# A new global order and new buffer slots for the tasks of an attention and feed-forward kernel

## The chip, the cores and the metric

One core of a Trainium2 chip. The time of a run is the device time of one execution in microseconds. In the profile PE is TensorE (PEld its weight loads), DVE is VectorE, ACT is ScalarE, POOL is GpSimd and SP is SyncE, which here does nothing but start transfers.

## The reference

Attention over 4 batches, 8 heads, 768 positions and 64 dimensions per head, and on its result x (3072 tokens of 512 features) a gated feed-forward layer of width 1536:

```
mask   = causal                         for heads 0, 2, 6
       = causal and (in the last 64 or among the first 4)   for the others
a      = softmax(mask(q k^T / 8));   x = a v, heads side by side
g      = x @ w_gate;   gelu = 0.5 g (1 + erf(g / sqrt(2)))
ffn    = (gelu * (x @ w_val)) @ w_out
out    = x + sigmoid(x @ w_res) * ffn
```

## The kernel before

The 3072 tokens are worked in six chunks of 512 (CHUNKS, called chunk 0 to 5; a chunk may join the end of one batch and the start of the next). For a chunk, q, k and v are loaded by POOL's queue with a cast to 16 bits (`ld`, line 539). Features of q and k are brought onto the partitions by TensorE transposes and a copy for the first chunks (`qkT` line 682, `qkE` line 693), by DMA transposes on SP's queue for the later ones (`dT`, line 726); some of the results are copied once more by SP (`q6`, line 737), and parts of v too (`vs`, lines 617 and 633). Then come the scores (line 850), exp on ACT (line 866), masks on DVE (line 902), the products with v (lines 477, 478, 974) and the division by the row sum (`rcp` line 1028, `norm` and `norm16` lines 1039 to 1048), which gives x twice, in 32 and in 16 bits. x is turned to features by TensorE (`xT`, line 1063, and a copy `xE`, line 1071) and, in one block of chunks 3 to 5, by a DMA transpose on SP's queue (`xD`, line 1054). Gate and value products (`g`, `v`) follow, erf-gelu and product (lines 1098 to 1228), and the products with w_out (`fw`; for part of the gate, value and w_out products sums of blocks are formed first, so that seven products do the work of eight; lines 1151 to 1331), the residual gate (`res`, `tanh` line 1299), `gated` (line 1355), `add` (line 1365) and the output. In chunks 1 to 4, x itself is stored first (`xst`, line 1281, SP) and the rest is added to it in memory by an accumulating transfer of POOL (`out`, line 1359); a buffer of x is written again only after its store.

Matmul helper lines: 477 uses the whole array; 478 works in two halves of 64 columns, two instructions for one of line 477. Which form is used follows from the mode of the array where a task stands.

All of this is a graph of 1861 numbered tasks. `schedule()` does not search: it goes through the list PLAN, one global order in which each number is a task, and appends the task to the list of its engine. A letter behind a number picks the engine where a task may run on several (a ACT, d DVE, g POOL, s SP). `wN` stands for N fillers: matmuls of 128x256 on a zero tile whose result nobody reads (line 1414). PLACES says for each buffer, in the order of the tasks, which slot of its pool it takes; a task that takes a slot waits for the users of the buffer that had it. `assign_waits()` derives the semaphore waits, and each engine then runs its list strictly in order:

```
for x in "".join(PLAN).split():
    if x[0] == "w":
        for _ in range(int(x[1:])):
            t = next(fillers)
            t.bufs[0].fixed = t.bufs[0].pool.quiet("warm")
            if t.bufs[0].fixed is not None:
                place(t, "pe")
    else:
        t = self.tasks[int(x.rstrip("padgs"))]
        place(t, {"p": "pe", "a": "act", ...}[x[-1]] if x[-1] in "padgs" else t.eng)
```

Some numbers used below: 0 to 17 constants and masks; 199 to 204 the thirds of w_gate and w_val, 205 w_res, 206 to 209 w_out; 210 to 215 q and k of chunk 0, 216 to 219 its v; 244, 245, 254, 255 q and k of chunk 1; 302 a `dT` and 334, 335 `q6` copies of chunk 3; 522 and 538 gate matmuls of chunk 0; 973 `xst` of chunk 2; 1175, 1181, 1199 `norm` and `norm16` tasks of chunk 3, 1201 and 1203 its `xT`, 1183 its `xD`; 1819, 1851 and 1852 final `add` tasks.

Of the kernel before, what the change touches and what calls it, by code (L numbers as in the profile page):

```python
# [51 lines left out]
    "1 0 14 214 16 210 211 212 215 2 5 w39 240 213 241d w2 228 216 229a w4 230 236 231d 217 237d w6 411 3 6 232 412 4 233d "  # L52
    "200 w4 408 242 409 7 w1 234 243d 238 8 235a 9 239d 10 219 w5 414 410 w1 476 415 11 222 425 416 223 419 224d 426 221 "
    "420 417 422 218 418 225d 427 428 478 421 459 423 477 220 429 424 199 430 w3 442 460 443 413 471 444 431 245 445 432 "
    "472 w1 449 446 447 433 450 255 451 464 462 448 465 434 452 201 453 463 w4 467 461 202 13 435 468 w4 455 436 479 480 "
    "481 466 203 457 456a 437 w1 438 440 458a 482 439d 204 441d w1 473 226d w1 523 474 483 454 205 539 484 538 475 254 227d "
    "522 485 244 503 470 524 505 469 504 540 252 525 207 506 486 541 496 253a 497 488 507 498 206 499 487 514 500 489 501 "
    "266 516 490 17 530 491 267a 256 494 511 531 495d 246 532 492 515 493d 208 502 509 546 508 510a 552 512d 247 533 534 "
    "517 554 209 536 527 556 257 542 558 268 547 548 280 553 550 281 549 526 551 269 555 528 570 529 535 543 537 572 15 576 "
    "594 574 578 544 588 580 545 577 598 559 557 571 590 582 573 584 575 579 586 561 560 564 562 610 592 563 566 581 264 "  # L60
    "568 250 611 265d 296 518 290 589 520 251d 565 287 567 519 289 569 262 198 690 521 295 687 691 12 679 248 591 599 259a "
    "277 680 583 593 585 276 602 688 621 597 293 587 612 622 332 689 670 261a 676 671 674 326 600 249 613 605 623 283 675 "
    "260d 606 624 603 677 625 272 682 595 626 271 681 685 667 601 686 683 284 668 607 672 678 263 614 292 615 684 669 627 "
    "274 632 628 673 616 275 609 617 629 322 692 696 618 697 636 286 633 638 637 634 693 640 639 604 694 641 635 695 698 "
    "714 715 699 642 608 643 258d 700 644d 713 645a 703 701 704 705 649 706 702a 646 707 647 716 718 596 650 648a 709 708 "
    "717 711 710a 652 719 651 722 720 723 653 712d 724 721a 655 725 656 654 740 726 741 727 730 658 731d 728 659 657 729a "
    "747 619 746 660 620 735 770 734 630 742 736 664 631 771 737 273 738 772 752 661 744 754 739 743 662 748 732 745 774 "
    "750 278 663 749 756 775d 785 270 773 776a 777 751 786a 753 787a 755 778 282 796 779 797a 788 781 758 789 799 297 798a "
    "760 800 790 782 792 780 294 757 801 784 793 791 803 783 802 795 285 804 759 794 806 807 762 761 291 808d 805 818 763 "
    "809a 810 829 819d 288 764 811 830a 820d 821 398 831a 812 822 832 813 814 279 328 823 833 824 299 825 306 834 815 298 "  # L70
    "836 835 329 816 826 837 827 848 817 300 828 838 766 320 849 839 765 768 307 767 665 931 397 769 850 343 840 932 852 "
    "844 853 304 851 841 922 856a 924 308 906 845 925 858 847 859 309 843 854 860a 855 842 301 923 864 857d 865 316 846 910 "
    "907 866 926 861 870 911 871 862 914 927 863 928 875 867 929 874 868 909 876 881 310d 908 915 917 912 869 317 882 877 "
    "913 916 342 918 872 934 935 303 936 937 920 878 919 331 942 933 921 938 879 873 939 940 885a 943 323 944 318 880 887 "
    "945 888 946 941a 325 956 952 883 889a 930 957 958 319 884 947 948 953 333 959 949a 954 955 950 960 963 951a 961 965 "
    "315 964 893 886a 966 962a 894 967 330 890 312a 891 313d 895 971 892 969 972a 899 968 666 896 970a 314 897 900 305 976 "
    "1011 981 898 975 327 977 978 979 982 302 980 984 988 311d 1013 983 1012 1015 324 1014 985 987 986 989 990 345 1016d "
    "991 1026 973 992 1018 1027a 993 1017a 995 334 1019 1029 321 904 997 1037 1020 1038a 1021 1022 1028a 994 1030 1039a "
    "1023 903 1040 1024 1031 905 1041 996 1025 1032 998 1042 1048 1033 1000 1044 335 1049a 1034 1045 1035 1043 999 1036 "
    "1046 1051 1001 1047 1050d 1059 1052 1003 1070 1060d 1002 901 1061a 1062 1071a 1054 902 1063 1072a 1005 1004 1064 360 "  # L80
    "1073 1066 1053 1065 1074 336 1007 1055 1075 337 1056 1077 1067 1076 1058 1068 371 1078 1089 1069 1079 347 1009 1057 "
    "1006 1090 358 1008 1080 733 1091 369 1010 384 1166 1081 1093 1167 383 1085 1094 1082 1092 1153 400 1151 1097d 1154 "
    "1159 1095 1086 357 1099 1084 1152 1100 1083 361 1096 1101a 1156 1088 1098a 1163 394 1157 1087 1105 1106 404 1102 1164 "
    "1107 1103 1158 1111 1112 1160 1104 1147 1116 1161 1115 1108 1148 1109 1155 1117 1118 1110 1162 1149 340 1188 1150 1177 "
    "1119 1168 1113 349 1178 1122 1165 1173 1169 1170 1171 350 1179 1172 1189 1184 1185 1120 1174 1180 368 1175 1123 1181 "
    "372 1121 1186 1190 1195 1126d 401 1191 365d 1187 1176d 1124 1125 1192 1114 1183 1182 1197 1128 1127a 1129 1193 1196 "
    "1131 1130a 1198 1132 1194a 370 1199 1134 1135 1133 1203 1136 1201 338 1137 1204d 1202a 1138 1140 1139 1141 1200 1219 "
    "373 1214 1142 1208 1243 1143 1213 359 1145 1220 1245 339 1244 1215 1216 1217 346 1207 1218 1221 354 1222 1246 1223 "
    "1209 355 1210 1224 1211 385 1231 1212 1258 395 1269 1259a 1247 348 1270a 1225 1260a 1248d 1271a 1227 1249d 1250 344 "
    "1272 1251 1261 1233 1273 367 1252 1262 1235 1253 1254 351 1263 1144 1264 1265 1255 1274 1257 1226 366 1276 1266 1206 "  # L90
    "1256 1275 399 1268 1229 1228 1267 1280 1277 341 1281d 1237 1279 1230 1239 974 1282a 1291 1278 352 1283 1238 1292a 1284 "
    "356 1302 1293d 1294 1303a 1285 1295 1240 1241 1205 1287 1305 1304a 1296 1242 1286 353 1306 1288 380 1297 1298 1308 "
    "1289 376 1307 1299 1309 1321 1146 1301 1290 1300 1310 379 1232 1322 1312 1234 388 1311 1402 1323 392 1236 1403 1317 "
    "403 1325 1313 1324 1326 377 363d 1387 1314 1329a 1385 1399 1386 1327 1318 1388 1331 364d 1316 1332 1328 1320 1400 "
    "1333d 1379 1383 1315 1337 1330a 374 1380 1338 1319 1334 381 1401 1335 1384 1339 1393 1390 1381 1343 1336 396 1391 1344 "
    "1382 1404 1340 1348 1405 362a 1389 1406 1394 378 1407 1408 1409 1341 1410 1354 1411 1355 1413 1342 405 1412a 1397 "
    "1358d 1395 1392 1415 1396 1414 1356 1416 1360 1417 1361 1398 1357 1347 1419 1420 1424 1362d 1359a 1349 1425 1418 1421 "
    "1422 1423 1426 1427 1366 1428 1363 1429 375 1367 1364 1430a 1368 1431 1365 1432 1433 1372 1434 1369 1435 1370 1373 "
    "1371 1437 1439 1438a 1350 1440d 1436 1444 1351 1481 1450 1345 1452 1374 1455 1346 1443 1479 513 1445 391 1446 1447 382 "
    "1449 1448 1461 1375 1451 1480 1457 1453 389 1483 1454 1463 1484a 1456 1459 1485d 1486 1465 1458 1487 1679 1494 1442 "  # L100
    "1460 1462 1495a 1482 1488 1464 1490 1489 1496d 1491 1466 1497 1493 1505 390 1498 1467 1492 1499 1506a 1469 1501 386 "
    "1508 1507d 1471 1500 1509 1441 1502 1516 1503 402 1510 1517a 1511 1504 1518a 1468 1512 1519 393 1527 1520 1470 1528a "
    "1513 1529a 1472 1521 1530 387 1515 1522 1523 1514 1473 1531 1524 1538 1525 1533 1539a 1526 1475 406 1532 1540d 1477 "
    "1541 1474 1534 407 1542 1476 1535 1543 1536 1352 1545 1537 1478 1544 1353 1549 1640 1546 1377 1557 1376 1548 1378 1641 "
    "1559 1547 1558 1550 1633 1560 1621 1631 1553 1634 1561 1552 1562 1563 1554 1565a 1564 1556 1632 1567 1551 1568 1566d "
# [1405 lines left out]
```

## Time and profile before

| | |
|---|---|
| median of 3 runs | 266.2 us (265.41 to 267.15) |
| profiled execution | 264.3 us, span from its first to its last instruction |
| granted TensorE clock, mean | 0.997 |
| PE busy | 254.5 us (96%), 3421 matmuls |
| DVE busy | 210.8 us (80%), 473 instructions |
| ACT busy | 155.3 us (59%), 274 instructions |
| POOL busy | 106.8 us (40%), 145 instructions |

The profiled execution has its span as its only time. Busy time counts an engine's computation; issuing a DMA counts on POOL and not on SP. Times are microseconds from the span's start; a matmul of a row x8 is one of eight that overlap, so the step from one to the next is shorter than its duration.

### The profile page before, as it was taken

How to read it: one execution, taken by the hardware profiler on the slowest of the kernel's cores; microseconds unless marked ns; L12 is line 12 of the kernel's file. 1: busy time of each engine (PE TensorE's matmuls, PEld its weight loads, DVE VectorE, ACT ScalarE, POOL GpSimd, SP SyncE). 2: the span in 40 equal slices, each digit the busy share in tenths (PEclk: the TensorE clock that was granted, in tenths of full speed). 3: DMA queues.
4: the chain of work that ended last, by engine and by line, in shares of the span. 5: the costliest groups of instructions: out<-in, count | busy, mean ns of one | idle time of the engine just before them, and what ended most of it. 6: DMA issues, size and time to landing. Idle time of an engine off the chain costs nothing.

```text
span 264.3 us, 8077 instructions
## 1 busy us (share of the span) xinstructions
PE 254.5 (96%) x3421; PEld 180.7 (68%) x3421; DVE 210.8 (80%) x473; ACT 155.3 (59%) x274; POOL 106.8 (40%) x145
## 2 busy tenths in 40 slices
PE   8999999999999999999998899999999998999993
PEld 5657655558567578667677477579588677778891
DVE  1499555999988978678999677999687976877985
ACT  1277534964554998564883356884655995445511
POOL 8996741990000998013976620711500111110021
PEclk9999999999999999999999999999999999999998
DMA  7999999999297999968999994899589509050004
GB/s 69 166 139 178 207 196 191 188 158 115 82 271 99 141 123 135 182 154 182 136 97 124 152 138 93 200 123 104 69 92 237 101 2 122 7 77 2 2 2 159
DMA packets 102067, 33.17 MB, mean 125 GB/s; under 512 B 88720, under 2 KB 97168, under 8 KB 102032
## 3 DMA queue, kind: packets, MB, share of 16 engines
q0 software_dynamic: 74704, 18.88, 77.3%
q1 hardware_dynamic: 26896, 13.26, 25.0%
q8 instruction: 27, 0.44, 0.7%
q10 hardware_dynamic: 432, 0.52, 0.5%
q14 instruction: 8, 0.07, 0.1%
HBM read 29.36 MB, written 10.49 MB: 151 GB/s over the span
## 4 chain that ended last, share of the span: by engine, by line
PE 87%; DVE 8%; DMA 3%; issue 1%; ACT 0%; DVEq 0%
PE ps L477 45%; PE ps L478 30%; PE ps L850 4%; PE ps L1414 4%; DMA xT<-x 3%; PE ps L682 2%; PE ps L974 2%; PE ps L1063 1%; DVE xtok L1041 1%; DVE x L1039 1%; DVE vk L598 1%; PE ps L941 1%; DVE hS L1251 0%; DVE hT L1228 0%; DVE vs L617 0%
## 5 line engine op out<-in xcount | busy, mean ns | idle before, releaser
L539 POOL DMA_DIRECT2D qks<-in_q_dram x37 | 33.2, 983 | 48.3 <-DMA qT<-qks 26.1
L1359 POOL DMA_DIRECT2D out_dram<-otile x16 | 15.6, 975 | 76.8 <-DVE otile L1355 66.2
L477 PE MATMUL ps<-xT,wg 128*128 128x512 f16 (+1 forms) x172 | 38.7, 337 | 1.4 <-DMA xT<-x 1.0
L477 PE MATMUL ps<-xT,wv 128*128 128x512 f16 (+1 forms) x172 | 38.5, 337 | 0.0
L1129 ACT ACTIVATE gact<-ps 128x512 f16<-128x512 f32 x38 | 22.1, 596 | 27.0 <-PE ps L477 18.0
L1131 DVE SCALAR_TENSOR_TENSOR hT<-gact,ps 128x512 f16<-128x512 f16 x38 | 25.8, 683 | 13.7 <-ACT gact L1129 5.8
L539 POOL DMA_DIRECT2D qks<-in_k_dram x37 | 34.8, 977 | 1.4 <-POOLq L1493 0.8
L1203 DVE TENSOR_TENSOR ps<-ps,otile 128x256 f32<-128x256 f32 x60 | 24.0, 428 | 7.7 <-PE ps L477 3.7
L1221 ACT ACTIVATE gact<-ps 128x512 f16<-128x512 f32 x30 | 16.6, 596 | 15.7 <-PE ps L477 10.8
L539 POOL DMA_DIRECT2D va<-in_v_dram x24 | 23.7, 1017 | 3.8 <-DVE va L534 3.8
L477 PEld LDWEIGHTS ps<-xT,wg 128*128 128x128 f16 x172 | 16.2, 98 | 13.1 <-DMA xT<-x 1.5
L477 PEld LDWEIGHTS ps<-xT,wv 128*128 128x128 f16 x172 | 16.6, 98 | 11.4 <-issue 0.2
L866 ACT ACTIVATE ea<-ps 128x1024 f16<-128x1024 f32 (+2 forms) x24 | 22.0, 925 | 1.4 <-PE ps L850 1.3
L1228 DVE SCALAR_TENSOR_TENSOR hT<-gact,ps 128x512 f16<-128x512 f16 x30 | 19.3, 682 | 2.6 <-PE ps L478 1.2
L1299 ACT ACTIVATE srs<-ps 128x512 f32<-128x512 f32 x22 | 13.1, 599 | 12.2 <-PE ps L478 7.8
L477 PE MATMUL ps<-wo,hT 128*128 128x256 f16 (+1 forms) x114 | 18.3, 296 | 0.0
L478 PE MATMUL ps<-xT,wg 128*64 128x512 f16 (+1 forms) x144 | 17.6, 344 | 0.0
L478 PE MATMUL ps<-xT,wv 128*64 128x512 f16 (+1 forms) x144 | 17.6, 344 | 0.0
L1041 DVE TENSOR_TENSOR xtok<-ps,rcp 128x512 f32<-128x512 f32 (+1 forms) x28 | 16.8, 608 | 0.6
L1331 DVE TENSOR_TENSOR otile<-otile,ps 128x256 f32<-128x256 f32 x33 | 13.1, 412 | 3.7 <-PE ps L477 2.4
L850 PE MATMUL ps<-qT,kT 64*128 64x64 f16 (+4 forms) x391 | 15.9, 213 | 0.1
L478 PE MATMUL ps<-wo,hT 128*64 128x256 f16 x216 | 15.6, 273 | 0.4 <-DVE otile L1325 0.4
(175 smaller groups left out, 590.4 us busy)
## 6 DMA issues: line engine op xcount, KB each, us to landing
out_dram<-xtok SPq DMA_DIRECT2D x4, 1024.0 KB, 4.8
out_dram<-otile POOLq DMA_DIRECT2D x16, 256.0 KB, 4.5
va<-in_v_dram POOLq DMA_DIRECT2D x24, 128.0 KB, 5.6
qks<-in_k_dram POOLq DMA_DIRECT2D x32, 64.0 KB, 4.9
qks<-in_q_dram POOLq DMA_DIRECT2D x32, 64.0 KB, 5.0
wv<-in_moe_w_val_dram POOLq DMA_DIRECT2D x3, 512.0 KB, 13.2
wg<-in_moe_w_gate_dram POOLq DMA_DIRECT2D x3, 512.0 KB, 11.4
wo<-in_moe_w_out_dram POOLq DMA_DIRECT2D x4, 384.0 KB, 20.9
```

The lines of the kernel that those rows point to most:

```text
L477: return e.matmul(o, lhsT=lhsT, rhs=rhs, **k)
L478: return [e.matmul(o[h:h + 64], lhsT=lhsT[:, h:h + 64], rhs=rhs, **k) for h in (0, 64)][-1]
L539: return G.add(eng, issue, lambda e: e.dma_start(out_ap(), in_ap), deps, prio, bufs=bufs, dma=cost, name=name, grp=grp)
L850: return [e.matmul(at(scr)[:, oo:oo + w], lhsT=side(BB, qb, low, 1)[half, k0:k0 + 128], rhs=side(BB, qb, low, 0)[half, qq:qq + w], start=T ...
L866: return e.activation(out=o, in_=i_, func=AF.Exp, scale=SM_SCALE)
L1041: t2 = G.add("dve", c_dve(2 * n * 64), lambda e: e.tensor_tensor(out=xview(), in0=avv(0, DHEAD), in1=scale(), op=ALU.mult), [t1] + xdeps, ...
L1129: ta = G.add("act", c_act(512), (lambda gb=gb, ga=ga, gw=gw: lambda e: e.activation(out=at(ga)[:, :], in_=at(gb)[:, gw], func=AF.Gelu))(), ...
L1131: th = G.add("dve", c_dve(512), (lambda vb=vb, ga=ga, f=f, vw=vw: lambda e: e.scalar_tensor_tensor(out=hv(f), in0=at(ga)[:, :], scalar=0.5 ...
L1203: return G.add("dve", c_dve(256), lambda e: e.tensor_tensor(out=at(ps)[:, o], in0=at(ps)[:, BL], in1=at(es)[:, 0:256], op=ALU.add), deps, ...
L1221: ta = G.add("act", c_act(512), (lambda x=x, ga=ga, both=both: lambda e: e.activation(out=two(at(ga)[:, :]), in_=both(x), func=AF.Gelu))() ...
L1228: th = G.add("dve", c_dve(512), (lambda x=x, f=f, ga=ga, both=both: lambda e: e.scalar_tensor_tensor(out=two(hv(f)), in0=two(at(ga)[:, :]) ...
L1359: t = G.add("pool", 1.0, (lambda ot=ot, r0=r0: lambda e: e.dma_start(out[r0:r0 + 128, :], at(ot)[:, :], accum_op=ALU.add))(), ends + [stor ...
```

## The change

PLAN and PLACES are replaced; nothing else in the program differs. Both orders contain the same numbered tasks except for fillers. In words of the order: 48 fillers in place of 77, the first group 25 in place of 39. The list of loads on POOL has another order: the loads of q and k of chunk 1 (244, 245, 254, 255) all stand ahead of the weights 201 to 205. Of SP's transfers, `xst` of chunk 2 (973) and the `dT` and `q6` of chunk 3 (302, 334, 335) come later in the order, and of the two DVE tasks that feed `xD` (1183) the last is now 1181 (`norm16`) and was 1176 (`x16`, a cast). Of the final additions two (1819, 1851) run on DVE in place of POOL. DVE has ten instructions fewer, ACT 13 more, POOL two fewer, SP one fewer. 28 more value matmuls and 16 more residual-gate matmuls are in the two-halves form (14 and 8 fewer in the full form).

```diff
--- before.py
+++ after.py
@@ -49,85 +49,84 @@
...
 PLAN = (
-    "1 0 14 214 16 210 211 212 215 2 5 w39 240 213 241d w2 228 216 229a w4 230 236 231d 217 237d w6 411 3 6 232 412 4 233d "
-    "200 w4 408 242 409 7 w1 234 243d 238 8 235a 9 239d 10 219 w5 414 410 w1 476 415 11 222 425 416 223 419 224d 426 221 "
-    "420 417 422 218 418 225d 427 428 478 421 459 423 477 220 429 424 199 430 w3 442 460 443 413 471 444 431 245 445 432 "
-    "472 w1 449 446 447 433 450 255 451 464 462 448 465 434 452 201 453 463 w4 467 461 202 13 435 468 w4 455 436 479 480 "
-    "481 466 203 457 456a 437 w1 438 440 458a 482 439d 204 441d w1 473 226d w1 523 474 483 454 205 539 484 538 475 254 227d "
-    "522 485 244 503 470 524 505 469 504 540 252 525 207 506 486 541 496 253a 497 488 507 498 206 499 487 514 500 489 501 "
-    "266 516 490 17 530 491 267a 256 494 511 531 495d 246 532 492 515 493d 208 502 509 546 508 510a 552 512d 247 533 534 "
...
-    "1011 981 898 975 327 977 978 979 982 302 980 984 988 311d 1013 983 1012 1015 324 1014 985 987 986 989 990 345 1016d "
-    "991 1026 973 992 1018 1027a 993 1017a 995 334 1019 1029 321 904 997 1037 1020 1038a 1021 1022 1028a 994 1030 1039a "
...
-    "1119 1168 1113 349 1178 1122 1165 1173 1169 1170 1171 350 1179 1172 1189 1184 1185 1120 1174 1180 368 1175 1123 1181 "
-    "372 1121 1186 1190 1195 1126d 401 1191 365d 1187 1176d 1124 1125 1192 1114 1183 1182 1197 1128 1127a 1129 1193 1196 "
-    "1131 1130a 1198 1132 1194a 370 1199 1134 1135 1133 1203 1136 1201 338 1137 1204d 1202a 1138 1140 1139 1141 1200 1219 "
...
-    "1801 1835 1803a 1834d 1804 1789 1836 1805 1837a 1838 1806d 1839 1793 1807 1840 1841 1842 1849 1844 1851g 1843 1808 "
...
-    "1818 1812 1819g 1797 1816 1859a 1817 1821 1822 1820s 1823d 1824a "
+    "0 212 198 213 1 14 16 17 215 2 w25 234 232 233 235a w5 414 419 416 5 210 420 415 211 w5 228 229a w3 230 238 242 243a "
+    "214 6 217 231 15 216 408 239 409 245 236 237a 240 241 3 411 412 422 423 459 7 460 218 8 4 225 9 410 244 10 467 11 224 "
+    "425 426 418 427 219 428 429 417 430 w5 476 220 468 w2 471 199 478 421 477 424 413 431 472 221 464 449 461 223 442 432 "
+    "226 465 222 443 450 451 444 445 200 473 433 469 474 434 462 446 452 447 435 255 463 w3 252 453 436 448 254 227a 438 "
+    "466 439 470 250 440 454 496 441 475 251a 437 457 458a 479 201 203 455 480 497 498 253a 456 499 481 500 482 503 504 501 "
+    "483 522 502 484 530 505 506 204 485 202 524 538 532 486 507 487 488 489 514 511 490 531 516 205 257 540 512 509 510 "
+    "492 493 539 494 533 246 247 523 525 495a 266 508 518 520 541 491 515 517 256 534 543 542 526 264 536 265 544 528 267a "
+    "207 519 535 521 558 537 560 562 527 679 206 680 13 545 12 208 209 546 564 570 588 572 576 574 552 577 579 566 578 580 "
+    "290 554 590 559 561 529 581 563 594 589 591 571 592 556 598 573 575 593 289 346 286 582 548 259 584 568 674 667 296 "
+    "550 636 583 565 586 567 569 585 587 668 675 553 676 677 339 295 269 337 261 262 248 690 691 271 555 557 547 549 669 "
...
+    "1067 305 318 382 1073 1072 352 994 996 1068 1069 302 1147 1074 1148 1075 998 1076 397 335 1089 1090 1077 1078 1091 "
+    "1092 1081 1082 1079 1080 1156 1157 1161 1085 376 1093 1094 905 342 379 377 902 1162 334 1084 1083 1095 1096 1163 1166 "
...
+    "1110 1113 1190 513 1116 973 1173 400 1197 1185 1174 1155 1186 1187 1191 1118 1119 358 1120 380 1198 388 1121 1175 1122 "
+    "366 1176 1177 1192 1179 1123 1178 1193 1199 1180 1181 1124 1125 1126a 1127 1128 1129 1194a 1203 1117 367 1183 1200 "
...
+    "1845 1846 1805 1847 1806a 1848 1810 1809 1850 1811 1813 1794 1795 1852g 1856 1851 1858 1860 1814 1796 1797 1854a 1812 "
+    "1816 1817 1815 1818 1819 1853a 1822 1821 1820a 1823 1824a "
 )
 PLACES = (
...
 )
...
```

## Rows read from the trace of the kernel before

**Rows 1.** the page: busy time of the engines; the chain that ended last
```profile
PE 254.5 (96%) x3421; PEld 180.7 (68%) x3421; DVE 210.8 (80%) x473; ACT 155.3 (59%) x274; POOL 106.8 (40%) x145
...
PE 87%; DVE 8%; DMA 3%; issue 1%; ACT 0%; DVEq 0%
```

**Rows 2.** five stretches: busy us of each engine (instructions), PEclk, DMA share, GB/s
```profile
13.70:23.70 10.00, 9.30 (x152) 5.96 (x151) 9.56 (x29) 7.84 (x17) 9.96 (x14) 1.00 1.43 145
23.70:124.00 100.30, 100.30 (x1054) 65.88 (x1055) 81.31 (x184) 63.57 (x111) 43.29 (x56) 1.00 1.35 165
124.00:150.00 26.00, 24.23 (x305) 17.07 (x303) 22.02 (x49) 15.88 (x25) 19.59 (x26) 1.00 1.46 115
150.00:262.00 112.00, 108.16 (x1781) 82.91 (x1779) 93.65 (x205) 64.51 (x118) 21.82 (x27) 1.00 0.61 92
220.00:227.00 7.00, 5.94 (x200) 5.76 (x196) 4.90 (x12) 2.86 (x6) 0.00 (x0) 1.00 0.65 88
```

**Rows 3.** PE's timeline of the start: start us, us, work, [idle before <- releaser]
```profile
1.21 7.03 PE L1414 MATMUL ps<-blank 128*128 128x256 f16 x39 [1.21 <-DVE blank L511]
...
23.67 0.71 PE L477 MATMUL ps<-xT,wg 128*128 128x256 f16 x5 [0.38 <-DVE xtok L1041]
```

**Rows 4.** line 1414 up to 8.2 us: ns min/median/max of one
```profile
L1414 PE MATMUL ps<-blank x39: 272/421/421, 1.2 to 8.0; 128*128 128x256 f16 x39
```

**Rows 5.** DVE's timeline of the start, columns as in rows 3
```profile
14.61 0.52 DVE L508 COPY m_win<-m_win 128x256 f16<-128x256 f16 x1
...
23.10 0.42 DVE L1041 TENSOR_TENSOR xtok<-ps,rcp 128x256 f32<-128x256 f32 x1
```

**Rows 6.** POOL's timeline of the start
```profile
11.36 0.24 POOL L497 TENSOR_SCALAR_AFFINE_SELECT m_win<-m_win 128x64 f16<-128x64 f16 x1
11.55 0.91 POOL L539 DMA_DIRECT2D va<-in_v_dram  x1
...
14.79 0.75 POOL L539 DMA_DIRECT2D wg<-in_moe_w_gate_dram  x1
```

**Rows 7.** tile wg: us from issue to landing of its loads
```profile
DMA to landing us min/median/max: 7.5/11.4/15.0
```

**Rows 8.** the chain that ended last, in order of time, before chunk 3
```profile
141.80 0.64 DVE x L1048
142.46 7.36 DMA xT<-x
```

**Rows 9.** PE's timeline of the hand-over to chunk 3
```profile
143.20 0.82 PE L477 MATMUL ps<-wo,hT 128*128 128x256 f16 x6
144.74 0.61 PE L1063 MATMUL ps<-ident,x 128*128 128x128 f16 x8 [0.72 <-DVE x L1039]
...
149.86 0.61 PE L477 MATMUL ps<-xT,wg 128*128 128x512 f16 x2 [1.05 <-DMA xT<-x]
```

**Rows 10.** line 1054, the DMA transposes of x: us from issue to landing
```profile
DMA to landing us min/median/max: 3.7/4.9/7.4
```

**Rows 11.** SP's queue from 112 to 125 us
```profile
113.50 2.58 SPq L726 DMA_TRANSPOSE kT<-qks  x2
...
116.82 0.59 SPq L1281 DMA_DIRECT2D out_dram<-xtok  x1
```

**Rows 12.** PE's timeline around 223 us
```profile
223.98 0.44 PE L478 MATMUL ps<-vk,ek 128*64 128x65 f16 x16 [1.06 <-issue]
```

**Rows 13.** all engines' timeline of the tail
```profile
258.99 1.27 POOL L1365 TENSOR_TENSOR otile<-otile,xtok 128x512 f32<-128x512 f32 x1 [1.96 <-DVE otile L1355]
...
260.91 0.69 DVE L1365 TENSOR_TENSOR otile<-otile,xtok 128x512 f32<-128x512 f32 x1
```

**Rows 14.** the longest waits: engine, line <- releaser: us in total, times, longest
```profile
POOL out_dram L1359 <- DVE otile L1355: 66.2, 8, 15.9
```

**Rows 15.** PE's timeline of chunk 3's first scores
```profile
130.67 0.27 PE L850 MATMUL ps<-q 64*128 64x256 f16 x1
```

123 rows, old and new, of tables (PLACES, PLAN) are left out of this document.

## The prediction

> **What bounds the kernel now.** I read four views. First the busy totals and the chain that ended last [rows 1]: PE is busy 254.5 of 264.3 us, and 87% of the chain is PE. Both orders hold the same real tasks, so most of the time can't move. Second the stretches [rows 2]: PE is full from 23.7 to 124 us, loses 0.7 us between 13.7 and 23.7, 1.8 us around the change from chunk 2 to chunk 3 (124 to 150), and 3.8 us in all of 150 to 262. Third the timelines of what loses, by the idle time in brackets before PE's groups: 1.21 us at the start and 0.38 before the first gate matmul [rows 3], 0.72 and 1.05 at the hand-over to chunk 3 [rows 9], 1.06 at 223.98 [rows 12]; and in the tail 2.7 us of a last DMA after DVE's last addition, 260.91 + 0.69 = 261.60 [rows 13]. Fourth the fillers (line 1414), 77 of them, which keep PE at work where it would wait [rows 3, 4]; the new order has 48. A filler that covers a wait costs nothing by itself, but what shortens the wait lets it be dropped. So what an order can win is some of the 8 us of fillers at the start and 4 to 5 us of gaps; and any new wait between 23.7 and 124 us is paid whole.
>
> The sum is made against the profiled execution, 264.3 us, and 1.9 us are added for the median (266.2).
>
> **The start.** The first gate matmul of chunk 0 stands at 23.67 us, behind a DVE normalisation that began at 23.10 and ended at 23.52 [rows 3, 5]. DVE is busy 9.56 of the 10 us before [rows 2]; its chain from the mask copy of line 508 (14.61) to that norm is 23.52 - 14.61 = 8.9 us [rows 5]. The new order cuts the first fillers from 39 to 25. The 39 take 7.03 us [rows 3]: 25 slow ones (421 ns long [rows 4], a step of 0.21) and 14 fast ones (272 ns, a step of 0.11), so 25 end at about 6.5 us instead of 8.2. But DVE's chain is fed by the mask constants from POOL, of which the last ended at 11.36 + 0.24 = 11.60 [rows 6]. In the new order 11 loads are issued ahead of it instead of 9, at 0.75 to 0.91 us each [rows 6]: 11.60 + 2 x 0.85 = 13.3 us. From there the DVE tasks in front of the first gate matmul (now task 522) add up to 9.4 us by the durations that the same tasks had, so it comes at some 22.8 us, 0.8 us earlier. Ahead of it PE has done 0.7 us more real work than before (transposes and scores of chunk 1), which is saved later. Together **-1.5 us**. Bounds: -2.5, if DVE's chain isn't held by the constants; +0.5, if the landing of the first gate weights decides: their load was issued at 14.79 [rows 6] and the quickest of the three took 7.5 us [rows 7], so 22.3, only 1.4 us ahead of its use.
>
> **The weights behind it.** Two more loads of q and k of chunk 1 (254 and 244, 256 KB each) now stand ahead of the weights 201 to 205: 0.5 MB at 165 GB/s [rows 2] is 3.1 us of stream. Against it, the PE work ahead of each weight's first use grows by about as much, since PE does chunk 1's transposes earlier. Counted by bytes ahead and work ahead, each weight lands 1.3 to 3 us before its use; I put it at **0**, bounds 0 to +3, since PE has nothing else in line to hide a late weight behind.
>
> **The hand-over to chunk 3.** Before, PE stood 0.72 us for x of line 1039 and 1.05 us for the DMA transpose of x (line 1054) [rows 9], which was issued at 142.46 after a cast on DVE and took 7.36 us in the chain [rows 8]. The three of this kind took 3.7, 4.9 and 7.4 us [rows 10]. In the new order the feeder on DVE (1199) of the TensorE transposes (1203, 1201) is ahead of the other norm, and four final matmul groups lie in front of them: I let the 0.72 go whole. The DMA transpose (1183) now follows norm16 1181, DVE's sixth task after the norm 1175: 0.64 for the cast [rows 8], about 0.65 for each of three norms and 0.15 for each of two reciprocals, 2.9 us. PE reaches the last task that feeds 1181 about 1.05 us after 1175, so 1181 ends 1.85 us after that task. From there PE has 12 final groups of three matmuls (a step of 0.11 each, 0.33 a group [rows 9]), two transposes (0.22 each) and six gate and value groups (0.43 each) before it needs the result: 7.0 us. Less DVE's 1.85 that is 5.2 us. With a transfer of 4.9 us nothing waits; with 7.4 it is 2.2 us. I take 0.7, as many of POOL's loads have left that stretch: 1.77 becomes 0.7, **-1.1**, bounds -1.8 and +0.4.
>
> The shortest of the three transposes, 3.7 us, lies in a stretch in which POOL is busy 0.00 us; around the longest POOL is busy 19.59 of 26 us [rows 2, 10]. A rule of the Trainium skill ("DMA: Bandwidth & Descriptors", Issuing engines are not separate DMA queues) says that transfers run on the same 16 engines and interleave, whichever engine issued them; with that the trace agrees, and by the rule alone the emptier stretch would win the whole 1.77.
>
> **Later gaps.** The 1.06 us at 223.98 waited for nothing that the profile shows ("issue") [rows 12]; I take it as an even chance that it comes back somewhere. The 0.7 us of other small gaps behind DVE should be less, as DVE loses ten tasks and ACT gets 13. **-0.6**, bounds -1.5 and +0.3. The DMA transposes of chunks 4 and 5 have 7.2 and 7.5 us of PE work after their feeders, before 7.4 and 7.9: no wait at 3.7 to 4.9 us and 1 to 1.5 us of DVE.
>
> **The tail.** Two of the final additions move from POOL (1.27 us for 512 columns) to DVE, where one takes 0.69 [rows 13]. After PE's last matmul DVE has one addition more: **+0.3**, bounds 0 and +0.7.
>
> **Forms.** 28 more value matmuls and 16 more of the residual gate run on halves of the array, two for one, in place of 14 and 8 on the whole. Laid end to end by the steps that the tasks had, the real PE work is 241.9 us against 241.3: **+0.6**, bounds 0 and +1.
>
> **New waits.** 1861 tasks have new places, and the old order shows that several gaps of 0.2 to 1 us stay in one that looks smooth. **+0.6**, bounds 0 and +2 (one more hand-over like the old one).
>
> Sum: -1.5 + 0 - 1.1 - 0.6 + 0.3 + 0.6 + 0.6 = -1.7 us: span 262.6, median **264.5 us**. The terms' ends don't all meet; this case has 262.8 to 266.2 as its own range.
>
> **Rivals.** (1) *All gaps close*: start -2.5, hand-over -1.8, later gaps -1.2, no new wait: -2.5 - 1.8 - 1.2 + 0.3 + 0.6 = -4.6, **261.6 us**. Against it is DVE's chain at the start, which stays.
>
> (2) *It does not do what it says*: the transpose at the hand-over takes 7.4 us whatever lies beside it, so 2.2 us of wait (+0.4), and the start gains only the 0.7 us of work moved forward, no gap closes: +0.4 - 0.7 + 0.3 + 0.6 + 0.6 = +1.2, **267.4 us**; with new waits at 0, 266.8.
>
> (3) *Slower, by SP's queue before chunk 3.* Transfers of SP start in line. A copy of q (334) waits for a transpose (302) that was issued in the pair at 113.50 [rows 11]; the first scores of chunk 3 that read such a copy ran at 130.67, 14 us later [rows 15]. In the new order 302 waits for a load that stands on POOL behind two output transfers, and those wait for DVE (8 such waits, the longest 15.9 us [rows 14]). By the tasks ahead I place its landing at 120 to 122 us and the first scores of chunk 3 at 125 to 126: 3 to 6 us of room. The store of chunk 2's x (973), for which a norm of chunk 3 waits, is behind it. From a delay of 4.5 us on, each further us stands on PE. A POOL wait longer by half of that longest one, 8 us, gives 3.5 us: 266.2 + 3.5 less the 0.3 or so that the rest then still gains, **269.4 us**.
>
> (4) *Slower, by the clock.* The granted clock is 1.00 from 13.7 to 262 us, the 2.4 GHz level [rows 2]; but the first fillers ran 421 ns and the later ones 272 [rows 4], so PE began at 1.2 GHz and rose while 39 fillers stood back to back. Now 25 stand there, as many as were slow, and behind them come transposes and gaps. If the clock rises only with the dense matmuls, the 8 to 9 us of real work in the start take twice as long; some 5 us of fillers and waits take up the rest: +4 us on the forecast, **268.5 us**.
>
> On this the Trainium skill ("TensorE: Matmul & The Clock Gate", Part 4: PE-mode transpose) speaks against the change: a transpose on TensorE does not count as busy in the same way, so it does not raise the clock. In the trace of before the clock had risen ahead of the first transpose; no row here shows either.
>
> **Chances.** Forecast 0.48, rival 1 0.13, rival 2 0.20, rival 3 0.12, rival 4 0.07. A measurement of this kernel tells some 1% (2.66 us) from no change: faster is below 263.5, slower above 268.9. Faster: 0.13 and half of the forecast's case, 0.24: 0.37. Slower: rivals 3 and 4, less a little: 0.18. Within 1%: 0.45. The range goes from rival 1's middle (261.5) to short of rival 3's (269.0).
>
> **What would show it.** The first gate matmul at 22.5 to 23 us behind DVE; fillers of 272 ns before 9 us; PE full from there to 120 us; under 1 us idle at the hand-over and the transpose of x under 6 us; DVE's last addition 1.6 to 1.9 us after PE's end. The prediction is wrong if PE waits for a weight between 30 and 55 us, for a copied q or a norm at 120 to 140 us, or if the clock stays low.

## The result and the profile after

The changed kernel is slower: 269.86 us median of 16 runs against 265.54 for the kernel before, 1.0163 times as long by these medians, 1.0118 (interval 1.0089 to 1.0147) by the ratio without outliers; in a second series of runs 1.0207 (1.0155 to 1.0259). Every ratio with an interval leaves out the runs that lie over 1.5% above the fastest of the same kernel as disturbed, and since this kernel spreads from 266.6 to 273.6 us (and once 510), such a ratio is more a lower bound here, and the ratio of the medians of all runs stands beside it where the argument hangs on it. The profiled execution is one of the quick ones: 267.34 us, span 265.6, against a median of 266.2 and a span of 264.3 for the kernel before.

The page of the changed kernel, the lines that answer to [rows 1] (its line numbers are one lower):

```profile
PE 253.5 (95%) x3414; PEld 176.5 (66%) x3414; DVE 204.8 (77%) x463; ACT 163.0 (61%) x288; POOL 104.6 (39%) x143
...
PE 76%; DMA 11%; DVE 6%; SPq 3%; POOL 1%; issue 1%; ACT 0%; POOLq 0%; DVEq 0%
```

PE is busy 1.0 us less, and yet the kernel is slower. The chain names the new part: DMA has 11% of it in place of 3%, SP's queue 3% in place of nothing. The stretches, the same ones as in [rows 2], and one of 3.3 us behind the hand-over:

```profile
13.70:23.70 10.00, 8.64 (x172) 6.08 (x173) 9.88 (x34) 8.40 (x15) 9.87 (x16) 1.00 1.61 187
23.70:124.00 100.30, 99.33 (x1006) 63.89 (x1004) 77.31 (x172) 66.23 (x117) 51.70 (x67) 1.00 1.57 169
124.00:150.00 26.00, 24.02 (x318) 16.95 (x315) 20.39 (x46) 16.31 (x27) 17.91 (x22) 1.00 1.44 138
150.00:262.00 112.00, 110.24 (x1785) 81.97 (x1785) 92.21 (x202) 65.72 (x119) 12.65 (x15) 0.98 0.45 77
150.50:153.80 3.30, 3.30 (x10) 1.20 (x8) 1.71 (x5) 1.19 (x2) 0.65 (x2) 0.50 1.04 178
```

PE is no longer full between 23.7 and 124 us, where POOL and the DMA engines are busier (DMA share 1.57 against 1.35), and behind the hand-over the granted clock is 0.50, 1.2 GHz, for a while. Such a stretch can't be seen in busy time, where PE looks full: 10 matmuls ran in it. PE's timeline at three places, the start, a new wait and the hand-over:

```profile
1.13 5.52 PE L1413 MATMUL ps<-blank 128*128 128x256 f16 x25 [1.13 <-DVE blank L510]
...
22.92 1.04 PE L476 MATMUL ps<-xT,wg 128*128 128x256 f16 x8
```

```profile
97.26 1.89 PE L476 MATMUL ps<-wr,xT 128*128 128x512 f16 x8
100.09 0.22 PE L973 MATMUL ps<-vs,es 128*64 128x65 f16 x1 [0.94 <-DMA vs<-va]
```

```profile
150.11 0.76 PE L476 MATMUL ps<-xT,wg 128*128 128x512 f16 x2 [2.09 <-DMA xT<-x]
150.67 1.06 PE L476 MATMUL ps<-xT,wv 128*128 128x512 f16 x2
151.52 1.91 PE L476 MATMUL ps<-xT,wg 128*128 128x512 f16 x4
153.23 0.90 PE L476 MATMUL ps<-xT,wv 128*128 128x512 f16 x2
153.97 0.81 PE L476 MATMUL ps<-xT,wg 128*128 128x512 f16 x4
```

The first gate matmul comes at 22.92 in place of 23.67 [rows 3], close to the forecast of 22.8. Then a wait of 0.94 us near 100 us that the kernel before doesn't have, and at the hand-over one wait of 2.09 in place of 0.72 + 1.05 [rows 9]; behind it four gate matmuls take 1.91 us where four of the same form take 0.81 at the end of the rows. The chain that ended last, cut to the 21 us before the first of these waits ends, shows where it comes from:

```profile
79.78 0.89 POOL va L538
80.68 2.19 POOL qks L538 x3
82.87 8.32 DMA qks<-in_k_dram
91.19 0.02 issue
91.20 1.22 SPq L725
92.43 0.04 issue
92.47 7.57 DMA vs<-va
100.04 0.04 issue
100.09 0.83 PE ps L973 x40
```

Read upward: PE's windowed product of chunk 2 waits for a copy of v (task 278, `vs`, line 632), which SP started at 92.47. SP started it then because it stands in line behind the transpose 338 (91.20), and that waits for the load 336, which POOL issued at 82.87 and which landed 8.32 us later. The copy has nothing to do with that load: its own last input had landed at 77.7. And 338 prepares keys of chunk 4, whose first scores run near 169 us; in the kernel before, the copy started at 73.85 and 338 at 146. POOL issued 336 so late because a load five places ahead of it in POOL's order (304) waits for a transpose of chunk 2 to land (78.5).

Summed in this execution: PE ends at 260.18 + 0.82 = 261.00 against 259.30 + 0.84 = 260.14, so +0.86. Start -0.75; copy of v +0.94; hand-over 2.09 - 1.77 = +0.32; half of the 3.3 us at 0.50, +1.65; the gaps over 0.2 us behind 160 us, which were 0.31 + 0.40 + 1.06 + 0.21, are 0.24 + 0.41, -1.33. That makes +0.83. The tail adds 0.40 (DVE's last addition ends 1.86 us after PE, before 1.46). Together +1.2 of the +1.3 us of the span.

The three executions of the changed kernel that were profiled (this one and those of experiments 1 and 3) agree on this: their spans of 265.6, 266.3 and 267.5 us, less their waits at the two places (0.94 + 2.09, 3.27 + 2.33, 2.31 + 2.33) and less 1.65 where the clock fell behind them (the first and the third), leave 260.9, 260.7 and 261.2. The spans of experiments 6 and 9 below, which have neither wait, are 260.9 and 260.8. So to within 0.3 us the two waits and the clock behind them are what these executions lost, and without them the new order is 3.4 us ahead of the 264.3 of the kernel before (2.2 us by the medians in experiment 6).

### The profile page after: what moved, and what is told of

Same layout as the page of the kernel before. It is cut to its first block, busy times and chain, and to the rows that moved or that the text cites. A ratio compares the mean times of both kernels' runs of the same rounds, so it can differ in the third digit from the quotient of the medians.

```text
span 265.6 us, 8044 instructions
## 1 busy us (share of the span) xinstructions
PE 253.5 (95%) x3414; PEld 176.5 (66%) x3414; DVE 204.8 (77%) x463; ACT 163.0 (61%) x288; POOL 104.6 (39%) x143
## 4 chain that ended last, share of the span: by engine, by line
PE 76%; DMA 11%; DVE 6%; SPq 3%; POOL 1%; issue 1%; ACT 0%; POOLq 0%; DVEq 0%
PE ps L476 34%; PE ps L477 31%; PE ps L849 4%; DMA qks<-in_k_dram 3%; DMA xT<-x 3%; DMA vs<-va 3%; SPq L725 3%; PE ps L1413 2%; DMA kT<-qks 2%; PE ps L973 2%; PE ps L1062 2%; PE ps L681 1%; POOL qks L538 1%; DVE otile L1354 1%; DVE otile L1364 1%
## 5 line engine op out<-in xcount | busy, mean ns | idle before, releaser
L1358 POOL DMA_DIRECT2D out_dram<-otile x16 | 14.9, 1065 | 88.0 <-DVE otile L1354 47.7
L1202 DVE TENSOR_TENSOR ps<-ps,otile 128x256 f32<-128x256 f32 x60 | 25.0, 429 | 7.8 <-PE ps L477 3.0
L538 POOL DMA_DIRECT2D va<-in_v_dram x24 | 25.1, 1060 | 15.0 <-PE ps L973 11.7
L476 PE MATMUL ps<-wo,hT 128*128 128x256 f16 (+1 forms) x114 | 19.3, 295 | 0.0
L1325 ACT ACTIVATE otile<-ps 128x256 f32<-128x256 f32 x27 | 10.2, 390 | 14.4 <-PE ps L477 8.3
L477 PE MATMUL ps<-xT,wv 128*64 128x512 f16 (+1 forms) x152 | 18.8, 340 | 0.0
L849 PE MATMUL ps<-qT,kT 64*128 64x64 f16 (+4 forms) x391 | 17.1, 213 | 1.1 <-ACT es L865 0.4
```

Source lines behind the costliest of these rows:

```text
L476: return e.matmul(o, lhsT=lhsT, rhs=rhs, **k)
L477: return [e.matmul(o[h:h + 64], lhsT=lhsT[:, h:h + 64], rhs=rhs, **k) for h in (0, 64)][-1]
L538: return G.add(eng, issue, lambda e: e.dma_start(out_ap(), in_ap), deps, prio, bufs=bufs, dma=cost, name=name, grp=grp)
L849: return [e.matmul(at(scr)[:, oo:oo + w], lhsT=side(BB, qb, low, 1)[half, k0:k0 + 128], rhs=side(BB, qb, low, 0)[half, qq:qq + w], start=T ...
L1202: return G.add("dve", c_dve(256), lambda e: e.tensor_tensor(out=at(ps)[:, o], in0=at(ps)[:, BL], in1=at(es)[:, 0:256], op=ALU.add), deps, ...
L1358: t = G.add("pool", 1.0, (lambda ot=ot, r0=r0: lambda e: e.dma_start(out[r0:r0 + 128, :], at(ot)[:, :], accum_op=ALU.add))(), ends + [stor ...
```

## The experiments

Each is timed against the kernel before on the same chip; experiments 1 to 4 ran on one chip, 5 to 8 and 12 on a second, 9 to 11 on a third. The changed kernel has 1.0207 in the series of 1 to 4. Each profile is of one execution.

**1. The changed kernel again.**

> The changed kernel once more, unedited, for a second profile and more times. Theory A (a hand-over to chunk 3 that waits for the DMA transpose of x, and a TensorE clock that falls for it): the wait before the first gate group of that block is 1 to 3 us again, followed by a stretch of granted clock 0.5, and 267 to 270 us. Theory B (SP's queue in chunk 2: the copy of v, task 278, stands behind a transpose that waits for a late load): a wait of 1 us or more near 100 us, of another size than the 0.94 us of the first profile. Rival C (no fixed place, the loss moves about): the waits stand elsewhere and neither of these two is over 0.5 us.

268.04 to 271.89 us. PE's waits in its profile:

```profile
PE ps L973 <- DMA vs<-va: 3.3, 1, 3.3
PE ps L476 <- DMA xT<-x: 2.3, 1, 2.3
```

Both places again, the first 3.3 us long here: theory A and B, and not rival C. The clock stayed at 1.00, against theory A's second half.

**2. The copy of v ahead.**

```diff
-923 662 338 956 869 332 278 927 311a
+923 662 278 338 956 869 332 927 311a
```

> The changed kernel with one task moved: SP starts the copy of v (278) ahead of the transpose 338 instead of behind it. Theory B: the copy starts at about 88 us instead of 92.5, lands before 97, the wait of 0.94 us near 100 us is gone, and the time falls by 0.9 us against the changed kernel, more if that wait is larger in other executions. Theory A: nothing but that 0.9 us changes, the hand-over to chunk 3 still waits 1 to 3 us. Rival C: no change in the time beyond 0.5 us.

266.26 us, ratio 1.0028 (0.9995 to 1.006): one number moved takes 4.1 us off the median. SP's queue:

```profile
85.97 0.60 SPq L1370 DMA_DIRECT2D out_dram<-otile  x1
86.61 0.67 SPq L632 DMA_DIRECT2D vs<-va  x1
90.79 1.23 SPq L725 DMA_TRANSPOSE kT<-qks  x1
```

The copy starts at 86.61, the transpose waits as before, and PE has no wait at that place. The gain is far above the 0.94 us of the first profile, as theory B allows: that is the smallest of the three waits seen here (3.27 and 2.31 us in experiments 1 and 3). It is above the largest of them too; a clock that falls behind this wait, as in experiment 4 (0.50 from 102.9 to 106.1 us), adds to it.

**3. Fillers at the hand-over.**

```diff
-1141 1237 1209
+1141 1237 w18 1209
```

> The changed kernel with 18 more fillers (18 x 0.11 = 2.0 us) on PE just ahead of the gate group that waits for the DMA transpose of x. Theory A: the transpose lands when it did, so the gate group starts at the same time or up to 0.5 us later, but PE was not idle before it, the granted clock stays 1.00, and the dense matmuls behind it are not slowed: 1.7 us less than the changed kernel. If the clock has no part in it: the same time as the changed kernel, or up to 2 us more where the transpose lands early.

269.61 us, 1.0200. The trace holds 48 fillers, as the changed kernel: no bank of PSUM (the memory that takes the results of matmuls) was free at that point, and `schedule()` then leaves fillers out. So this is a third profile of the changed kernel and tells nothing of the clock: waits of 2.3 us at both places, the clock at 0.50 behind the second.

**4. The feeder first.**

```diff
-1178 1193 1199 1180 1181 1124 1125
+1178 1180 1181 1183 1193 1199 1124 1125
...
-1194a 1203 1117 367 1183 1200 1130a 1204a 1201 1131 1202 1182 1134 1132
+1194a 1117 367 1200 1130a 1131 1182 1134 1203 1204a 1201 1202 1132
```

(and in PLACES slot 0 in place of 2 for the reciprocal 1180)

> The changed kernel with the order on DVE at the hand-over as the kernel before had it: the norm that feeds the DMA transpose of x (1180, 1181) ahead of the two other norms (1193, 1199), so that the transpose starts 1.3 us earlier; the TensorE transposes of x stand two product groups later. Theory A: the wait of 2.1 us becomes 0.8 us or less, the clock does not fall, and the time is 2 to 3.5 us below the changed kernel. Theory B and rival C: at most 1.3 us below it.

267.83 us, 1.0105 (1.0056 to 1.0154). The wait for the transpose is gone, but another stands in its place:

```profile
148.06 0.50 PE L476 MATMUL ps<-wo,hS 128*128 128x256 f16 x3 [1.24 <-DVE otile L1324]
```

The two norms that were moved back now run late on DVE, and the copy 1127, which PE needs, behind them. Net 2.6 us on the median.

**5. Both.** The edits of 2 and 4 together.

> Both single edits together: the copy of v (278) ahead of the transpose 338 on SP, and the feeder of the DMA transpose of x first on DVE. If the two waits are separate mechanisms, their gains add: 4.1 and 2.6 us below the changed kernel gives about 263.7 us, 1 us or so below the kernel before; the wait near 100 us is absent, the one at the hand-over 1 us or less. If they are one delay that is only passed on, the time stays at the 266.3 us of the first edit alone.

264.69 us, 0.9996 (0.997 to 1.0022): level with the kernel before, 1 us short of the sum; the 1.2 us of DVE's copy is there. In this execution PE's transposes at 11.56 us also waited 1.76 us for a load of q, and the first gate matmul came at 24.21 in place of 22.92, though nothing in the start was changed.

**6. Copy ahead and three loads later.** The edit of 2, and

```diff
-1224 1239 384 1225 1259
+1224 1239 1225 1259
...
-1270d 1272 391 1254 1255
+1270d 1272 1254 1255
...
-1286 1142 403 1146 1278 1293
+1286 1142 1146 384 391 403 1278 1293
```

> The copy of v ahead on SP, and three of POOL's loads for chunk 5 (384, 391, 403), which were issued in the 3 us before the DMA transpose of x, put behind the output transfer 1146 (some 10 us later). If the transpose is slow because POOL's loads fill the engines ahead of it: it takes 5.5 to 6.5 us in place of 8.5, the wait at the hand-over falls from 2.6 to below 1 us, and the time is 1.5 to 3 us below the first edit alone (266.3). If its time is its own or comes from SP's further transposes behind it: still 7.5 to 8.5 us and no gain.

262.66 us, 0.9933 (0.9901 to 0.9965; by the medians of all runs 0.9919): faster than both kernels. The time to landing of the transpose of x (line 1053, 140 to 155 us) in the run with the copy alone; then POOL's timeline and the same time in this run:

```profile
DMA to landing us min/median/max: 8.5/8.5/8.5
```

```profile
137.39 2.07 POOL L1358 DMA_DIRECT2D out_dram<-otile  x2 [1.93 <-DVE rcp L1027]
138.60 2.42 POOL L538 DMA_DIRECT2D qks<-in_k_dram  x2
149.72 0.90 POOL L1358 DMA_DIRECT2D out_dram<-otile  x1 [8.70 <-DVE otile L1354]
150.34 1.20 POOL L538 DMA_DIRECT2D va<-in_v_dram  x1
```

```profile
DMA to landing us min/median/max: 6.0/6.0/6.0
```

Against experiment 2 nothing on SP or DVE was changed here, and the transpose took 6.0 us in place of 8.5; PE no longer waits for it. So the loads of POOL in front of it make it slow. This holds in all profiles: 4.9 to 6.0 us in the five kernels with these loads later (experiments 6, 7, 9, 10 and 11), 7.5 to 8.5 in the eight executions with the loads in front. They were for chunk 5, and SP took up the first of them at 173.0 us in the changed kernel, 30 us after its load.

**7. All edits**, those of 4 and 6 and the copies 298 and 299 ahead of 279 on SP.

> All edits together: copy of v ahead, feeder first, the three loads later, and the two copies of q and k of chunk 2 (298, 299) ahead of the copy 279 and the store 732 on SP. Separate mechanisms: 262 to 263.5 us, clearly below the kernel before, no wait of PE over 0.7 us between 30 and 250 us. Otherwise as the run with two edits.

264.79 us, 1.0005 (0.9977 to 1.0034), 2 us worse than experiment 6. Its waits are 1.2 us for DVE's copy (line 1324), which experiments 4 and 5 have too, and 0.9 for the copy of v. Once the loads are away, putting the feeder first has no wait left to remove (the transpose took 4.9 us) and costs its own; what the moved copies 298 and 299 cost was not run by itself.

**8. The load ahead.** Only

```diff
-817 816 304 824
+817 816 336 304 824
...
-922 303 336 920 846
+922 303 920 846
```

> SP's order as in the changed kernel, but the load 336, for which the transpose 338 and so all of SP's line waits, is issued on POOL ahead of the load 304, which waits for a transpose itself. If the copy of v is late because it stands in line behind the late load: 336 lands near 75 instead of 91 us, 338 and the copy start by 88 to 89 us, the wait near 100 us is gone and the time falls by about as much as with the copy moved (to some 266.5 us). If the moving of the copy helped by something else (fewer transfers side by side near 92 us): no more than 1 us below the changed kernel.

267.89 us. The medians of all runs give 1.0116; the ratio of 1.0034 (0.9995 to 1.0073) rests on the seven shortest of twelve. SP's order wasn't touched. SP's queue, and three stretches of its start:

```profile
87.05 3.33 SPq L725 DMA_TRANSPOSE kT<-qks  x1
90.42 1.74 SPq L632 DMA_DIRECT2D vs<-va  x1
```

```profile
4.20:14.30 10.10, 7.54 (x139) 5.06 (x137) 3.81 (x7) 5.28 (x11) 10.10 (x20) 1.00 1.73 151
14.40:21.10 6.70, 6.51 (x84) 3.96 (x86) 6.40 (x21) 5.02 (x10) 6.57 (x11) 0.50 1.56 180
21.20:30.00 8.80, 8.80 (x149) 7.22 (x144) 7.32 (x26) 6.11 (x11) 7.32 (x10) 1.00 1.44 199
```

The transpose starts at 87.05 and the copy at 90.42, 2 us earlier than in the changed kernel and 4 us later than in experiment 2: the late load does hold SP's line. But the copy took 10.1 us and landed at 100.5 (100.0, 102.6 and 101.4 in the three executions of the changed kernel), and PE's wait is only 0.33 us because PE came to it at 100.2 in place of 99.2, after a granted clock of 0.50 from 14.4 to 21.1 us that put the first gate matmul at 24.00 in place of 22.92. So this experiment agrees with theory B in SP's queue and in part in the time, 1.0207 to 1.0116; the proof by the wait itself is experiment 2. How often the low clock in the start comes isn't known.

**9. The copy further ahead.** Experiment 6 with 278 in front of 348.

> As the run with the copy ahead and the three loads later (262.7 us), but the copy of v (278) stands two transfers further ahead on SP, before the transpose 348 and the copy 314. There it landed only 0.9 us before PE needed it. If what is left of the spread comes from this copy being late in some executions, the median falls by 0.3 to 1 us and the highest run comes down; if not, the same time within 0.4 us.

264.75 us, 0.9952 (0.9922 to 0.9982), which rests on the nine shortest of twelve runs, and 0.9977 by the medians of all (highest run 269.05): no better than experiment 6. The copy started at 81.87 and landed 10 us ahead of use, and the spread is no smaller, so what is left of it isn't the copy's.

**10. The loads alone**, without the edit of 2.

> The changed kernel with the three loads of POOL later and nothing else: the fourth corner of the square of copy and loads. Two separate mechanisms: the transpose of x takes about 6 us, no wait at the hand-over, the wait near 100 us as in the changed kernel (0.9 to 3.3 us), 266 to 267 us. One mechanism: near 262.7 us, or no gain against the changed kernel's 270.

265.47 us, 0.9987 (0.9957 to 1.0017). The transpose took 5.5 us and nothing waited for it; the wait for the copy of v was 2.95 us, the other way round than in experiment 2: two mechanisms. The square is complete: neither 1.0207, copy 1.0028, loads 0.9987, both 0.9933. The two gains, 1.8% and 2.2%, add to 4.0%, and both edits give 2.7% (by the medians of all runs 1.6, 2.0 and 2.9%): they are not fully additive, and once the loads are away the copy is worth 0.5% (0.9% by the medians). The corners come from three chips. In this execution, too, PE's transposes waited for a load of q (1.19 us at 11.60), and the first gate matmul came at 24.10.

**11. The first fillers at 39.** Experiment 6 with `w25` changed to `w39`.

> As the run with the copy ahead and the loads later (262.7 us), with the first group of fillers at 39, as before, in place of 25. If the shorter group gained time at the start, as the prediction has it: the first transposes start 1.5 us later and the first gate matmul 0.3 to 1.5 us later, 263 to 264 us. If the start is set by the constants and DVE alone: the same time. If the shorter group costs clock (fillers that end before the clock is up for good): faster by 0.5 us or more and no low stretch in the first 25 us.

263.11 us, 0.993 (0.9908 to 0.9952): the same time. First gate matmul at 23.14, and here too a low clock from 15.1 to 18.3 us. The 14 fillers cost nothing that these runs show.

**12. Fillers that are placed.** The edit of 2, with

```diff
-1139 1141 1237 1209
+1139 1141 w18 1237 1209
```

and a change of `quiet()` that lets these 18 take a bank last used by DVE (its line numbers are five higher).

> The first edit (copy of v ahead on SP, 266.3 us) with 18 fillers (2.0 us) two products ahead of the gate group that waits for the DMA transpose of x, in a bank of PSUM that stands free there. If the wait costs twice, once as idle time and once by the fall of the clock behind it (1.7 us for each low stretch): the wait in front of the gate group shrinks to some 0.5 us, the granted clock stays 1.00 behind it, and the time falls by 1 to 1.7 us, though PE has done nothing useful. If the clock has no part in the time: the same time as with the first edit alone, or longer.

265.42 us, 0.9986 (0.9961 to 1.0012) against 1.0028 without the fillers: 0.4%, 1.1 us less, the intervals just overlapping. PE's timeline, and the stretch that read 0.50 without the fillers:

```profile
148.17 2.13 PE L1418 MATMUL ps<-blank 128*128 128x256 f16 x18
150.13 1.03 PE L481 MATMUL ps<-xT,wg 128*128 128x512 f16 x4
```

```profile
150.20:153.50 3.30, 3.30 (x19) 1.61 (x18) 2.62 (x6) 1.34 (x3) 0.35 (x1) 1.00 1.20 200
```

```profile
150.20:153.50 3.30, 3.30 (x9) 1.22 (x8) 1.48 (x4) 1.20 (x2) 1.13 (x2) 0.50 1.04 171
```

(The last row is experiment 2.) 19 matmuls against 9 in the same 3.3 us. It agrees with the wait that costs twice but doesn't show it: the intervals overlap, and in experiment 1 the clock stayed at 1.00 behind the same wait without fillers.

## Why the prediction was wrong

**The sign was wrong, and two terms made it so, with a cost behind them that wasn't priced.** The first is "New waits", +0.6 us. The place was not unknown: rival 3 is the mechanism, a transfer that stands in SP's line behind one that waits for a POOL load, itself behind waits on POOL. I looked for it only in front of chunk 3, where it didn't happen, and not for every transfer in SP's new order; it sits one chunk earlier, with a copy whose own inputs were there 15 us before it started. It measured 0.94, 3.3 and 2.3 us in three executions of the changed kernel, and removing it is worth 1.8% by itself, 0.5 to 0.9% where the loads of the hand-over are moved too. Rival 3's chance of 0.12 was that of one example, not of the whole queue.

**The second is the hand-over**, -1.1 us. The step that failed is "many of POOL's loads have left that stretch", from which I took 0.7 us of wait out of 0 to 2.2. The count of DVE's and PE's work was near: it gave 5.2 us of cover for the transfer, and 5.9 to 6.0 were there (transfers of 8.0 to 8.5 us, waits of 2.1 to 2.6). But the stretch had not emptied. POOL's loads around the transpose's start, before (start at 142.46) and after (142.05):

```profile
137.38 2.58 POOL L539 DMA_DIRECT2D qks<-in_q_dram  x3
139.59 1.12 POOL L539 DMA_DIRECT2D qks<-in_k_dram  x1
140.32 1.13 POOL L539 DMA_DIRECT2D qks<-in_q_dram  x1
141.05 1.14 POOL L539 DMA_DIRECT2D qks<-in_k_dram  x1
```

```profile
139.61 2.42 POOL L538 DMA_DIRECT2D qks<-in_k_dram  x2
141.14 1.78 POOL L538 DMA_DIRECT2D va<-in_v_dram  x1
142.01 2.40 POOL L538 DMA_DIRECT2D qks<-in_q_dram  x2
```

Five loads in place of six, and two of them beside the transpose; the prediction counted none of them. POOL was busy 17.91 of the 26 us where it had been busy 19.59, and the transfer was longer than any of the three before, not shorter. Rival 2 had the size, 2.2 us of wait, but not the reason: the transfer does depend on what lies beside it. The rule of the Trainium skill that I set beside it ("DMA: Bandwidth & Descriptors", Issuing engines are not separate DMA queues) is borne out by experiment 6, 8.5 to 6.0 us; it was its use, on a stretch that I took for empty, that was wrong.

**What wasn't priced: a wait that costs twice.** After such a wait the granted clock fell to 0.50 in some executions, 1.65 us in the profile above. I had the clock only as a rival of the start. In experiment 12, with PE kept busy in the wait, the clock stayed up, and its 1.1 us agree with the price, though the intervals overlap.

**Right in the number, not in the step: the start.** The first gate matmul was forecast at 22.8 us and came at 22.92, no matter whether 25 or 39 fillers stand in front (23.14 in experiment 11). But the mask constants, from whose end the 22.8 was reckoned, didn't hold DVE. POOL's last one, then DVE's work, in the changed kernel:

```profile
12.79 0.28 POOL L496 TENSOR_SCALAR_AFFINE_SELECT m_win<-m_win 128x64 f16<-128x64 f16 x1
```

```profile
12.87 0.69 DVE L692 COPY kT<-ps 128x512 f16<-128x512 f16 x1 [0.51 <-PE ps L681]
...
14.01 0.43 DVE L901 TENSOR_TENSOR ea<-ea,m_causal 128x512 f16<-128x512 f16 x1
14.36 0.53 DVE L507 COPY m_win<-m_win 128x256 f16<-128x256 f16 x1
```

The constants ended at 13.07, near the 13.3 that was reckoned, and DVE waited for none of them: it stood for PE's transposes (line 681) until 12.87 and then had work without a wait up to the first gate matmul. That this gave nearly the same time is luck. Where the transposes themselves waited for a load of q (experiments 5 and 10), the first gate matmul came at 24.1 to 24.2.

**Right, by its own steps.** The weights: no wait for one between 24 and 62 us (PE busy 38.27 of 38.30). Chunk 3's copied q and the norm behind the store of x: no wait. Tail +0.40 against +0.3. Later gaps -1.3 against -0.6. Forms and work moved forward: what is left of PE's +0.86 after the other terms is 0.03 us, against -0.7 and +0.6 that nearly cancel; neither is shown by itself. Rival 4 as put, a clock that doesn't rise before the dense matmuls, was in no profile; in two the clock fell in the start after it had risen, one of them with 39 fillers. Whether TensorE's transposes have a part in it, as the Trainium skill's rule has it ("TensorE: Matmul & The Clock Gate", Part 4: PE-mode transpose), no run here separates.

What stays open: why some waits of over 2 us were followed by a low clock and others not, what the load of q in the start waits for in some executions, and the rest of the spread, 261.6 to 265.1 us in experiment 6.

## What to carry to other kernels

In an in-order queue of transfers the question of each entry is not when its own inputs are ready but what stands ahead of it and what that waits for: a transfer that is needed 80 us later and waits for a late load must not stand ahead of one that is needed next. A transfer on the critical path is made shorter by keeping the loads that are not due yet out of the microseconds before it, with nothing changed on its own engine. A wait on PE is costed with the clock that may fall behind it, and from several executions, since one profile may hold the smallest of a wait that ranges over 2 us. And a forecast that meets its number is still read step by step: the start did, with another engine holding it.

## What I had not expected

Of nine waits of PE of over 2 us in these profiles (2.09, 2.31, 2.33, 2.33, 2.58, 2.58, 2.71, 2.95 and 3.27 us) five were followed by a granted clock of 0.50 and four were not, the longest (3.27) among these; after none of the waits of 1.6 us or less behind 30 us did it fall. And a copy of v on SP that took 5.6 and 4.4 us in the kernel before took 7.5 to 11.8 us where POOL's loads were dense, so that even a start 2.6 and 3.5 us earlier (experiments 7 and 12) left waits of 0.9 and 1.6 us in single executions.
